# Mixture-of-experts stage of an attention + MoE + FFN kernel: experts taken in an order sorted on the chip, each with a column width of its own, and weights laid out by partition

## The chip, the cores and the metric

One core of one Trainium2 chip runs the whole program. The metric is the device time of that core in microseconds (us). Unchanged, the kernel takes 641.47 us in the median of three runs (641.1 to 641.62).

## What is computed

Three layers follow each other on 1152 tokens of 512 numbers, in float32. First an attention in which each row keeps its 32 largest scores; its output `x` then goes through a mixture of eight experts, and that through a feed-forward layer. Cut to what matters here:

```python
logits = x @ w_gate                        # x is [1152, 512], w_gate [512, 8]
expert_idx = np.argmax(logits, axis=1)     # one expert for each token
gate_w = probs[np.arange(N), expert_idx]
...                                        # disp[e] = the tokens of expert e, in order; at most 288 each
h = np.maximum(np.einsum('ecd,edf->ecf', disp, w1), 0.0)   # w1 is [8, 512, 1024]
y = np.einsum('ecf,efd->ecd', h, w2)                       # w2 is [8, 1024, 512]
out[i] = gate_w[i] * y[expert_idx[i], pos[i]]
...
h = x @ w_in                               # the last layer, w_in [512, 2048]
g = h * np.clip(h + 3.0, 0.0, 6.0) / 6.0
return g @ w_out                           # w_out [2048, 512]
```

How many tokens an expert gets depends on the data. With the reference's inputs at its default seed the eight experts get 72, 137, 101, 181, 115, 186, 186 and 174 tokens.

## The kernel before, in words

The program has three stages one after the other. Within each, the order of the instructions on every engine is that of the source (`manual_schedule`): loops written out with hand-set positions, of which the ones used here are named below.

**Attention and routing.** 72 units (9 tiles of 128 tokens by 8 heads) pass through a software pipeline (`in_steps`). As tiles are done, `route` finds each token's expert (`oh`, one-hot) and its place among that expert's tokens (`pos`), and `send_rows` (L138) scatters the tokens' rows, scaled by their gate, into a DRAM buffer `xs` that holds 1152 rows for every expert. At step 16 the first expert's two weight matrices are loaded into two of three slots (`wslot`, 2 MB each, L600). At the end, for the last two tiles, the first expert's rows don't wait for the scatter: what has landed is read back (`load_first`, L187) and transposed into PSUM (`x_rows`, L161), the rest is added by a product with a 0/1 matrix (`pick0`, `x_pick`, L169), and VectorE copies the sum into `xe0` (`x_copy`, L158), on which the first expert starts. `most` (L512) keeps the count of tokens per expert (`sums`) and its maximum (`top_sum`).

**Experts.** The loop at L863 runs over 8 experts with 16 steps `m` each. `W = 192` columns (token places) are used for every expert. Steps 0 to 7 of an expert (phase a) make `hT = relu(w1' x)`, one 128-row block each, with four products (`hps`, L819), then ScalarE copies out (L827). Steps 8 to 15 (phase b) make the output (`yps`, L819), which ScalarE and VectorE write as a high and a low part into `x2h` and `x2l` at a column that is read from memory at run time (`nums`, L868, L836, L837). Each product of float32 numbers is two passes on TensorE, so an expert has 64 x 2 = 128 passes. In phase b the next expert's rows (`x_load`, L743) are transposed between the products (`turn`, `x_turn`, L153).

All loads are issued by SyncE (SP) in program order. Weight matrix n+3 is loaded into the slot of matrix n as soon as that one's phase is over (L872), so that two whole phases lie between a load's issue and its first use. Each load moves 128 lines: w1 in four pieces of 4 KB, w2 in eight of 2 KB. `x_load` of expert e+3 follows at the end of expert e. Beside these, from step 32 on, `conv_ticks` (L719) turns the last layer's weights, which come as 64-bit numbers, into pairs of float32 parts; one tick goes with every second step, and every third tick sends for the next 512 KB block (`load_raw`, L686): `w_in` blocks in pieces of 1 KB, `w_out` blocks in pieces of 4 KB. `finals` (L178) makes the columns at which the experts' outputs start, `compact` (L768) each token's column, and `check` (L783) sets `again` if an expert has more than 192 tokens or the selection of scores was not exact. If `again` is above 0, L970 runs everything once more in a slow form that has room for any input.

**Last layer.** `up` (L912) and `down` (L927) run over the 1152 columns, while the remaining weight blocks are converted. TensorE's products here have 384 or 512 columns.

Of the kernel before, what the change touches and what calls it, by code (L numbers as in the profile page):

```python
# [44 lines left out]
KW = 11  # L45
FILL = 4
# [11 lines left out]
def topk_attention_moe_ffn_kernel(ctx, tc, qT, kT, vx, vT, wg, w1, w2, w_in, w_out, out, cap):  # L58
# [17 lines left out]
    again = const.tile([1, 1], I32, name="again")  # L76

    def forward(fast):


        W = 192 if fast else cap
# [10 lines left out]
        top_sum = wp.tile([P, 1], F32, name="top_sum")  # L92
# [11 lines left out]
        if fast:  # L104
            x0, x0b, slot1 = (slots[2][:p, at:at + n] for p, at, n in
                              ((P, 0, DM), (W - P, DM, DM), (P, 3 * DM + W, W)))
            plain = slots[2][:, 4 * DM:5 * DM]
            xg_last = {t: wp.tile([P, DM], F32, name=f"xg{t}") for t in (NT - 2, NT - 1)}
            pick0 = {t: slots[2][:, at:at + W] for t, at in ((NT - 1, 3 * DM), (NT - 2, 6 * DM))}
        nload = [0]  # L110

        def load_w(name, part=0, parts=1):
            kind, e = name
# [32 lines left out]
        def x_turn(rows, x, psum):  # L146

            for g in range(2):
# [7 lines left out]
                x_copy(xp, g, x)  # L156

        def x_copy(xp, g, x):  # L158
            nc.vector.tensor_copy(x[:, 2 * g:2 * g + 2, :W], xp[:, :, :W])

        def x_rows(xp):  # L161
            for g in range(2):
                for i in range(2):
                    ks = slice((2 * g + i) * P, (2 * g + i + 1) * P)
                    for r, r0, n in ((x0, 0, P), (x0b, P, W - P)):
                        nc.tensor.matmul(xp[g][:, i, r0:r0 + n], r[:, ks], ident[:n, :n], is_transpose=True,
                                         start=False, stop=False)

        def x_pick(xp, xg, t, start=False, x=None):  # L169
            for g in range(2):  # L170
# [4 lines left out]
                if x is not None:  # L175
                    x_copy(xp[g], g, x)
# [10 lines left out]
        def load_first():  # L187
            nc.sync.dma_start(x0, xs[:P])
            nc.sync.dma_start(x0b, xs[P:W])

        with ExitStack() as actx:
# [74 lines left out]
            if fast:  # L266
                nc.gpsimd.iota(slot1, pattern=[[1, W]], base=1, channel_multiplier=0,
# [244 lines left out]
            def most(tot_p):  # L512
                v = nc.vector
                return [lambda: v.tensor_copy(sums[:, 0], tot_p),
                        lambda: v.tensor_reduce(top_sum, sums[:, 0], axis=AX.X, op=OP.max)]
# [45 lines left out]
            def in_steps():  # L561
# [80 lines left out]
                for f, *args in ((ptr, u - 2), (expo, u - 2), (attv, u - 3), (send, 4), (send, 5), (attv, u - 2),  # L642
# [6 lines left out]
                banks = [pool.tile([P, 2, 512], F32, name=name)[:, 0, :2 * W].rearrange("p (a w) -> p a w", a=2)  # L649
# [10 lines left out]
                    *most(tot)])  # L660
                x_rows(banks)
# [11 lines left out]
        with ExitStack() as mctx:  # L673
# [12 lines left out]
            def load_raw(n):  # L686
                f, j = divmod(n, 2)
                if f < NF:
                    r = raw[n % NRAW]
                    if j:  # L690
                        nc.sync.dma_start(r, w_out[f * P:(f + 1) * P])
                    else:
                        nc.sync.dma_start(r.rearrange("p (a f) -> p a f", a=HP),
                                          w_in[:, f * 2 * P:(f + 1) * 2 * P].rearrange("(a p) f -> p a f", p=P))
# [39 lines left out]
            with ExitStack() as ectx:  # L734
# [3 lines left out]
                PARTS = [(a, min(P, W - a)) for a in range(0, W, P)]  # L738
# [4 lines left out]
                def x_load(e):  # L743
                    xin[e] = []
                    for a, n in PARTS:
                        r = eb.tile([P, DM], F32, name=f"x{a}", bufs=2 + (a == 0))
                        if fast and n < P and e < 3:
                            nc.gpsimd.memset(r[n:], 0.0)
                        nc.sync.dma_start(r[:n], xs[e * NTOK + a:e * NTOK + a + n])
                        xin[e].append((r, a, n))  # L750

                def turn(e):
                    rows = xin.pop(e)
                    xe[e] = eb.tile([P, HP, W], F32, name="xe", bufs=1) if e % 2 else xe0
                    if fast:
                        return x_turn([(r, a, P) for r, a, n in rows], xe[e], two_banks)
                    return turn_one(rows, xe[e])

                def turn_one(rows, x):
                    for k in range(HP):  # L760
# [5 lines left out]
                        nc.vector.tensor_copy(x[:, k], xp)  # L766

# [15 lines left out]
                def check():  # L783
# [14 lines left out]
                    v.scalar_tensor_tensor(again_f, top_sum[:1], float(W), again_f, op0=OP.is_gt, op1=OP.add)  # L798
# [13 lines left out]
                class Expert:  # L812
                    def __init__(self, x, col):
                        self.x, self.col, self.y = x, col, {}
                        self.h = eb.tile([P, NFF, W], F32, name="hT", bufs=2 if fast else 1)

                    def products(self, out, wb, m, first, last):
                        for k in range(HP):
                            nc.tensor.matmul(out, wb[:, k], m[:, k], start=first and k == 0, stop=last and k == HP - 1)  # L819
                            yield  # L820

                    def use(self, wb, what):
                        if what[0] == "a":
                            f = what[1]
                            o = ps.tile([P, W], F32, tag="ps", name="hps")
                            yield from self.products(o, wb, self.x, True, True)
                            nc.scalar.activation(self.h[:, f], o, AF.Relu)  # L827
                            return
                        d, half = what[1:]
                        if half == 0:  # L830
                            self.y[d] = ps.tile([P, W], F32, tag="ps", name="yps")
                        o = self.y[d]
                        yield from self.products(o, wb, self.h[:, half * HP:(half + 1) * HP], half == 0, half == 1)
                        if half == 1:
                            cols = bass.ds(self.col(), W)
# [27 lines left out]
                for m in range(E * NP):  # L863
                    e, r = divmod(m, NP)
                    if r == 0:
                        ex = Expert(xe[e], lambda e=e: offv[e])
# [12 lines left out]
                    if fast and m == FIN:  # L879
                        finals()  # L880
                    if m == CPT:
                        compact()
# [139 lines left out]
```

## Time and profile before

| | us |
|---|---|
| median of 3 runs | 641.47 |
| the profiled execution | 639.62 |
| its span, first to last instruction | 637.8 |
| attention and routing, up to the first expert's product | 0 to 254.4 |
| experts | 254.4 to 427.4 |
| last layer | 427.4 to 637.8 |

The span is the profile's: 1.8 us of the execution lie around it. TensorE is busy for 609.8 us of it, VectorE for 375.5, ScalarE for 360.3, GpSimd for 311.3. In the profile PE is TensorE's matmul row, PEld its weight loads, DVE is VectorE, ACT ScalarE, POOL GpSimd, SP SyncE, and a small q marks an engine's own sequencer. A matmul's row ends when its result has drained, so rows of one stream overlap: the time between two starts, not the length of one row, is what a pass takes from the engine.

### The profile page before, as it was taken

What the parts mean: (1) busy time and instruction counts of PE and PEld (TensorE: products, weight loads), DVE (VectorE), ACT (ScalarE), POOL (GpSimd) and SP (SyncE); (2) the same over time, 40 slices, a digit from 0 to 9 for tenths busy, and PEclk for the clock granted to TensorE, in tenths of its full rate; (3) what the DMA queues carried; (4) which work ended last, traced back from release to release, by engine and by line L of the source; (5) the groups of instructions that cost most, each with busy time, mean ns of one, the idle gap of its engine ahead of it and who ended that gap; (6) DMA issues with size and microseconds to landing.
All of it is one profiled execution on the core that took longest, in us unless ns stands there. A gap on an engine that the chain in (4) does not pass through costs nothing.

```text
span 637.8 us, 12077 instructions
## 1 busy us (share of the span) xinstructions
PE 609.8 (96%) x4096; PEld 549.2 (86%) x4096; DVE 375.5 (59%) x1765; ACT 360.3 (56%) x687; POOL 311.3 (49%) x380
## 2 busy tenths in 40 slices
PE   8999999999888879999999999999999999999994
PEld 4888889888777767999999999999999999999993
DVE  5999999999999994002333323427665664222220
ACT  5999999989999963121334334336555553242221
POOL 7999999979999953001244222124234322030001
PEclk9999999999999979999999999999999999999998
DMA  8549600100000002885889887422222310020001
GB/s 268 168 134 386 212 17 2 35 2 18 18 18 19 2 1 95 293 290 148 306 264 280 276 308 239 165 64 85 81 85 84 97 34 1 1 99 1 1 1 54
DMA packets 36598, 74.13 MB, mean 116 GB/s; under 512 B 4016, under 2 KB 12464, under 8 KB 36528
## 3 DMA queue, kind: packets, MB, share of 16 engines
q1 hardware_dynamic: 34800, 68.55, 32.7%
q0 software_dynamic: 1728, 4.72, 2.0%
q8 instruction: 34, 0.56, 0.3%
q14 instruction: 36, 0.29, 0.2%
HBM read 63.83 MB, written 9.44 MB: 115 GB/s over the span
## 4 chain that ended last, share of the span: by engine, by line
PE 52%; DVE 24%; issue 15%; POOL 6%; ACT 1%; DMA 1%; DVEq 0%; SPq 0%; POOLq 0%; ACTq 0%
PE hps L819 13%; PE yps L819 13%; PE h L916 8%; PE acc L930 7%; DVE lists L342 7%; DVE lists L360 5%; DVE l L369 4%; DVE tops L371 3%; PE av L426 2%; POOL s L356 2%; PE ps L321 2%; PE pt L408 2%; POOL out_dram L939 1%; PE pt L566 1%; PE mix L443 1%
## 5 line engine op out<-in xcount | busy, mean ns | idle before, releaser
L342 DVE MAX8 lists<-s 128x8 f32<-128x72 f32 x576 | 118.6, 220 | 4.1 <-ACT s L326 4.1
L426 PE MATMUL av<-vt,pts 128*128 128x96 f32 (+1 forms) x800 | 100.5, 275 | 0.0
L916 PE MATMUL h<-x2h,fw 128*128 128x384 f32 x384 | 98.3, 336 | 0.9 <-DVE x2l L837 0.9
L426 PEld LDWEIGHTS av<-vt,pts 128*128 128x128 f32 (+1 forms) x800 | 92.1, 184 | 2.1 <-issue 0.9
L356 POOL TENSOR_TENSOR s<-s,cut 128x576 f32<-128x576 f32 x72 | 92.0, 1277 | 3.6 <-ACT cut L353 3.5
L819 PE MATMUL yps<-hT,wslot 128*128 128x192 f32 x512 | 90.9, 326 | 0.0
L930 PE MATMUL acc<-fw,gh 128*128 128x512 f32 x288 | 89.6, 392 | 0.0
L348 POOL TENSOR_TENSOR s<-s,lists 128x576 f32<-128x576 f32 x72 | 83.6, 1162 | 6.1 <-DVE lists L342 3.8
L408 PE MATMUL pt<-ident,ub 128*128 128x128 f32 x360 | 72.6, 287 | 13.5 <-POOL ub L385 7.9
L819 PE MATMUL hps<-xe,wslot 128*128 128x192 f32 x512 | 84.6, 326 | 0.2 <-DVE sc L184 0.2
L819 PEld LDWEIGHTS hps<-xe,wslot 128*128 128x128 f32 x512 | 83.4, 190 | 0.7 <-issue 0.7
L819 PEld LDWEIGHTS yps<-hT,wslot 128*128 128x128 f32 x512 | 82.1, 190 | 1.2
L408 PEld LDWEIGHTS pt<-ident,ub 128*128 128x128 f32 x360 | 50.8, 141 | 33.6 <-POOL ub L385 16.4
L916 PEld LDWEIGHTS h<-x2h,fw 128*128 128x128 f32 x384 | 70.5, 188 | 5.1 <-DVE x2l L837 1.2
L409 PE MATMUL pt<-drop,lb 128*128 128x128 bf16 x360 | 65.7, 220 | 0.0
L916 PE MATMUL h<-x2l,fw 128*128 128x384 f32 x192 | 64.7, 337 | 0.0
L930 PEld LDWEIGHTS acc<-fw,gh 128*128 128x128 f32 x288 | 53.4, 188 | 9.0
L919 ACT ACTIVATE g<-h,three 128x384 f32<-128x384 f32 x48 | 27.9, 581 | 55.7 <-PE h L916 55.7
L920 DVE SCALAR_TENSOR_TENSOR g<-g,h 128x384 f32<-128x384 f32 x48 | 26.5, 551 | 54.3 <-ACT g L919 53.9
L394 ACT ACTIVATE lb<-s,tops 128x576 bf16<-128x576 f32 x71 | 55.0, 775 | 4.9 <-DVE tops L371 2.8
L924 DVE TENSOR_TENSOR gl<-g,gh 128x384 fp32r<-128x384 f32 x48 | 27.4, 571 | 51.0 <-ACT gh L923 51.0
L923 ACT CAST gh<-g 128x384 fp32r<-128x384 f32 x48 | 24.7, 515 | 57.5 <-PE acc L930 52.9
(393 smaller groups left out, 1057.2 us busy)
## 6 DMA issues: line engine op xcount, KB each, us to landing
wslot<-in_w_dram SPq DMA_DIRECT2D x15, 2048.0 KB, 9.3
raw<-in_w_in_dram SPq DMA_DIRECT2D x16, 512.0 KB, 5.0
raw<-in_w_out_dram SPq DMA_DIRECT2D x16, 512.0 KB, 3.6
xs<-x_tok SPq DMA_DIRECT2D x8, 576.0 KB, 13.1
vt<-in_vx_dram SPq DMA_DIRECT2D x8, 365.0 KB, 3.6
kt<-in_kT_dram SPq DMA_DIRECT2D x8, 288.0 KB, 4.5
vts<-in_vT_dram SPq DMA_DIRECT2D x8, 288.0 KB, 3.8
qt<-in_qT_dram SPq DMA_DIRECT2D x9, 256.0 KB, 4.2
```

The lines of the kernel that those rows point to most:

```text
L342: yield lambda c=c: nc.vector.max(lists[t % 2][:, h, c], st[u][:, c * CW:(c + 1) * CW])
L348: nc.gpsimd.tensor_tensor(s2, s, lists[t % 2][:, h, :NCK, KEEP:].to_broadcast([P, NCK, CW]), op=OP.subtract)
L356: nc.gpsimd.tensor_tensor(st2[u], st[u], cuts.pop(u), op=OP.subtract)
L360: nc.vector.max(lists[t % 2][:, h, NCK], st2.pop(u))
L394: nc.scalar.activation(lbufs[u % 2][:, :S], st.pop(u), AF.Relu, bias=tops[t][:, h, TOPK - 1:], scale=-1.0)
L408: nc.tensor.matmul(pt[:, c], ubufs[u % 2][:, cs], ident, is_transpose=True, start=True, stop=False)
L409: nc.tensor.matmul(pt[:, c], lbufs[u % 2][:, cs], drop, start=False, stop=True)
L426: nc.tensor.matmul(av[t, g][rows, h % 4], pts[:, c, cols], vt[b, h // 2][:, at:at + VC], start=c == 0, stop=c == 4)
L819: nc.tensor.matmul(out, wb[:, k], m[:, k], start=first and k == 0, stop=last and k == HP - 1)
L916: nc.tensor.matmul(h2, fw[f][:, 0, a, k * P:(k + 1) * P], (x2h, x2l)[b][:, k, c * CH:(c + 1) * CH], start=n == 0, stop=n == len(ops) - 1)
L919: nc.scalar.activation(g, h2, AF.Relu, bias=three)
L930: nc.tensor.matmul(acc[j], g[a][:, j * P:(j + 1) * P], fw[f][:, 1, b], start=f == 0 and n == 0, stop=f == NF - 1 and n == 2)
```

## The change

The experts' order and widths change, and the layout of the weights in DRAM.

- `order()` sorts the eight experts by token count on VectorE, right after the counts are known. Expert 0 stays first (its weights are loaded long before); the other places take, by `PLACES`, the largest, the smallest, the second largest, the second smallest and so on. It writes the experts' numbers by place into `eids`.
- Place j has `WIDTHS[j]` columns: 176, 192, 132, 192, 140, 188, 152, 176, together 1348, where before there were 8 x 192 = 1536. Products, copies and row loads of a place use its width. With the inputs named above the places hold 72, 186, 101, 186, 115, 181, 137 and 174 tokens. `check` compares each place with its own width.
- Since the expert of a place is known at run time only, SP reads its number from `eids` (`who(j)`, one register load for each of the places 1 to 7) and the loads of weights and rows take their address from that register.
- The host lays `w1` and `w2` out so that what one partition gets is one line of 16 KB, and `w_in` so that its blocks come in lines of 4 KB.
- Small tables are filled on GpSimd at the start (10 instructions more), `finals_fast` and `compact_fast` take the sorted order into account, and the rows that fill up a row tile are cleared whole (128 rows, not the last 64).

```diff
+WIDTHS = (176, 192, 132, 192, 140, 188, 152, 176)
+PLACES = (0, 1, 7, 2, 6, 3, 5, 4)
...
-        W = 192 if fast else cap
+        Ws = WIDTHS if fast else [cap] * E
+        W, W0 = max(Ws), Ws[0]
...
         def load_w(name, part=0, parts=1):
-            src = (w1 if kind == "a" else w2)[e]
-            n = src.shape[1] // parts
+            n = 4096 // parts
             cols = slice(part * n, part * n + n)
-            nc.sync.dma_start(t.rearrange("p (a b) -> p a b", b=src.shape[1])[:, :, cols],
-                              src.rearrange("(a p) f -> p a f", p=P)[:, :, cols])
+            nc.sync.dma_start(t[:, cols], (w1 if kind == "a" else w2)[one(j), :, cols])
+        def one(j):
+            return bass.ds(eid[j], 1) if j in eid else j
...
+        def order():
+            v = nc.vector
+            v.scalar_tensor_tensor(keys, sums[:, 0], float(E), rank, op0=OP.mult, op1=OP.add)
+            v.max(places, keys)
+            v.tensor_copy(keys_in := sizes, places)
+            for j, at in enumerate(PLACES):
+                if j != at:
+                    v.tensor_copy(places[:, j:j + 1], keys_in[:, at:at + 1])
+            v.tensor_copy(whole, places)
+            v.tensor_scalar(eids, whole[:1], E - 1, E - 1, op0=OP.bitwise_and, op1=OP.bitwise_xor)
...
             def most(tot_p):
-                return [lambda: v.tensor_copy(sums[:, 0], tot_p),
-                        lambda: v.tensor_reduce(top_sum, sums[:, 0], axis=AX.X, op=OP.max)]
+                return [lambda: nc.vector.tensor_copy(sums[:, 0], tot_p)]
...
                     *most(tot)])
+                order()
                 x_rows(banks)
...
-                        nc.sync.dma_start(r[:n], xs[e * NTOK + a:e * NTOK + a + n])
+                        nc.sync.dma_start(r[:n], by_expert[one(j), a:a + n])
...
-                            nc.tensor.matmul(out, wb[:, k], m[:, k], start=first and k == 0, stop=last and k == HP - 1)
+                            nc.tensor.matmul(out, wb[:, k], m[:, k, :self.w], start=first and k == 0, stop=last and k == HP - 1)
...
+                def who(j):
+                    if fast and j < E:
+                        eid[j] = nc.values_load(eids[0:1, j:j + 1], engines=(mybir.EngineType.SP,), min_val=0,
+                                                max_val=E - 1)
                 if fast:
+                    who(1)
                     load_w(stream[2], 0, 2)
                     x_load(1)
                     load_w(stream[2], 1, 2)
+                    who(2)
...
                         if e + 3 < E:
+                            who(e + 3)
                             x_load(e + 3)
...
+    rows_first = lambda w: w.reshape(E, -1, P, w.shape[2]).transpose(0, 2, 1, 3).reshape(E, P, -1)
```

How the change moves VectorE's instructions at the end of the routing: the stretch from the count of tokens to the copy of the first expert's rows. `xe` is the first expert's input, `ps` and `pt` the two PSUM banks it is summed in. Before:

```order
L514 COPY sums<-tot_p 128x8
L515 TENSOR_REDUCE top_sum<-sums 128x1
L491 TENSOR_SCALAR rd<-cm 128x1
L492 TENSOR_TENSOR ra<-pos_p,oh 128x8
L493 TENSOR_REDUCE pr<-ra 128x1
L494 TENSOR_TENSOR dest<-rd,pr 128x1
L159 COPY xe_86<-ps 128x384
L159 COPY xe_86<-pt 128x384
```

After the change the eleven instructions of `order()` stand before the two copies, and one reduction is gone:

```order
L551 COPY sums<-tot_p 128x8
L529 TENSOR_SCALAR rd<-cm 128x1
L530 TENSOR_TENSOR ra<-pos_p,oh 128x8
L531 TENSOR_REDUCE pr<-ra 128x1
L532 TENSOR_TENSOR dest<-rd,pr 128x1
L193 SCALAR_TENSOR_TENSOR keys<-sums,rank 128x8
L194 MAX places<-keys 128x8
L195 COPY sizes<-places 128x8
L198 COPY places<-sizes 128x1 x6
L199 CAST whole<-places 128x8
L200 TENSOR_SCALAR eids<-whole 1x8
L171 COPY xe_93<-ps 128x2x176
```

The copies of the first expert's rows moved behind the sort on VectorE, and each of them has 352 columns where it had 384.

How it moves SP's queue at the start of the experts (`in_w` stands for the experts' weights, `x` for an expert's rows). Before:

```order
L189 DMA wslot_89<-xs 64x512
L121 DMA wslot_89<-in_w_dram 128x4x512
L749 DMA x_4196<-xs 128x512
L749 DMA x_4198<-xs 64x512
L121 DMA wslot_89<-in_w_dram 128x4x512
L693 DMA raw_4183<-in_w_in_dram 128x4x256
```

With the change:

```order
L222 DMA wslot_96<-xs 48x512
L897 TENSOR_LOAD eids
L897 ISA x2
L128 ISA
L128 DMA wslot_96<-in_w_dram 128x2048
L784 ISA
L784 DMA x_4233<-xs 128x512
L784 ISA
L784 DMA x_4235<-xs 64x512
L128 ISA
L128 DMA wslot_96<-in_w_dram 128x2048
L897 TENSOR_LOAD eids
```

A register load that waits for the sort now stands ahead of the second expert's weights, and a short address instruction (ISA) ahead of every load whose expert is found at run time; the order of the loads themselves is the same.

## Rows read from the trace of the kernel before

**Rows 1.** Experts: stretch, length, PE/PEld/DVE/ACT/POOL busy (instructions), clock, DMA share, GB/s.
```profile
254.40:427.40 173.00, 172.99 (x1081) 171.49 (x1081) 50.34 (x117) 55.36 (x141) 39.07 (x43) 1.00 0.74 243
```
**Rows 2.** Line L819, the experts' products: weight loads and matmuls, ns min/median/max.
```profile
L819 PEld LDWEIGHTS hps<-xe,wslot x512: 186/190/191, 254.4 to 416.5; 128*128 128x128 f32 x171
L819 PE MATMUL hps<-xe,wslot x512: 326/326/401, 254.4 to 416.7; 128*128 128x192 f32 x171
```
**Rows 3.** Chain of waits around the third expert: start us, us, what, how many.
```profile
298.03 10.40 PE hps L819 x64
308.43 0.33 PE yps L819 x2
308.76 0.11 PE xp L153
...
312.03 7.80 PE yps L819 x48
```
**Rows 4.** Attention's products of 96 columns, ten passes in order of time.
```profile
228.06 1.31 PE L426 MATMUL av<-vt,pts 128*128 128x96 f32 x10
```
**Rows 5.** The same products and their weight loads, among the page's costliest groups.
```profile
L426 PE MATMUL av<-vt,pts 128*128 128x96 f32 (+1 forms) x800 | 100.5, 275 | 0.0
...
L426 PEld LDWEIGHTS av<-vt,pts 128*128 128x128 f32 (+1 forms) x800 | 92.1, 184 | 2.1 <-issue 0.9
```
**Rows 6.** VectorE in order of time, end of the routing.
```profile
250.30 0.16 DVE L515 TENSOR_REDUCE top_sum<-sums 128x1 f32<-128x8 f32 x1
250.37 0.14 DVE L491 TENSOR_SCALAR rd<-cm 128x1 f32<-128x1 f32 x1
...
250.62 0.16 DVE L493 TENSOR_REDUCE pr<-ra 128x1 f32<-128x8 f32 x1
250.82 0.16 DVE L494 TENSOR_TENSOR dest<-rd,pr 128x1 int32<-128x1 f32 x1
252.95 0.56 DVE L159 COPY xe<-ps 128x384 f32<-128x384 f32 x1 [1.97 <-PE ps L173]
```
**Rows 7.** TensorE behind the experts' last product, in order of time.
```profile
424.81 2.60 PE L819 MATMUL yps<-hT,wslot 128*128 128x192 f32 x15
428.28 0.62 PE L916 MATMUL h<-x2h,fw 128*128 128x384 f32 x2 [0.87 <-DVE x2l L837]
```
**Rows 8.** SP's DMA issues at the start of the experts, in order of time.
```profile
253.64 0.38 SPq L121 DMA_DIRECT2D wslot<-in_w_dram  x1
259.51 0.85 SPq L749 DMA_DIRECT2D x<-xs  x2
```
**Rows 9.** The row loads issued at 259.5 (second expert), issue to landing.
```profile
DMA to landing us min/median/max: 2.8/2.8/2.8
```
**Rows 10.** Register loads of line L868, ns min/median/max.
```profile
L868 ACTq TENSOR_LOAD <-nums x8: 275/279/477, 265.1 to 417.1; - x8
```
**Rows 11.** The weight load (w1) issued at 298.1, issue to landing.
```profile
DMA to landing us min/median/max: 12.0/12.0/12.0
```
**Rows 12.** The weight load (w2) issued at 286.8, issue to landing.
```profile
DMA to landing us min/median/max: 8.3/8.3/8.3
```
**Rows 13.** Busy time of the experts at places 2, 3, 4 and 6 (columns as in rows 1).
```profile
297.70:319.50 21.80, 21.80 (x139) 21.62 (x138) 7.29 (x21) 6.49 (x17) 4.84 (x7) 1.00 0.78 236
319.50:341.20 21.70, 21.70 (x138) 21.53 (x137) 7.71 (x17) 8.75 (x21) 9.28 (x12) 1.00 0.91 278
341.20:362.90 21.70, 21.70 (x139) 21.52 (x138) 7.39 (x16) 7.82 (x20) 6.03 (x6) 1.00 0.93 292
...
384.60:406.30 21.70, 21.70 (x138) 21.53 (x138) 7.67 (x17) 8.75 (x21) 5.08 (x4) 1.00 0.79 267
```
**Rows 14.** End of the attention: where the clock fell, and after (columns as in rows 1).
```profile
226.00:232.70 6.70, 3.82 (x57) 3.66 (x58) 6.18 (x22) 4.52 (x10) 4.87 (x6) 1.00 0.01 2
232.70:239.60 6.90, 6.34 (x33) 5.82 (x33) 6.66 (x46) 4.09 (x7) 1.32 (x3) 0.51 0.00 0
...
247.00:254.40 7.40, 5.99 (x45) 4.29 (x45) 4.85 (x27) 1.71 (x4) 1.09 (x2) 1.00 0.25 89
```

More of the change, by code (lines that the diff above doesn't have):

```diff
@@ L45 @@
 KW = 11
+FRONT = 1 << 14
+WIDTHS = (176, 192, 132, 192, 140, 188, 152, 176)
+PLACES = (0, 1, 7, 2, 6, 3, 5, 4)
 FILL = 4
@@ L91, in forward @@
         sums = wp.tile([P, 3, E], F32, name="sums")
-        top_sum = wp.tile([P, 1], F32, name="top_sum")
+        rank, places, most_of = (wp.tile([P, E], F32, name=name) for name in ("rank", "places", "most_of"))
+        keys, sizes, starts = (wp.tile([P, E], F32, name=name) for name in ("keys", "sizes", "starts"))
+        whole = wp.tile([P, E], I32, name="whole")
         gates = wp.tile([P, NT, 1], F32, name="gates")
@@ L144, in send_rows, with x_turn @@
             return sd
-        def x_turn(rows, x, psum):
+        def x_turn(rows, x, psum, w=W):
             for g in range(2):
@@ L175, in x_pick, with finals_fast @@
                 if x is not None:
-                    x_copy(xp[g], g, x)
+                    x_copy(xp[g], g, x, W0)
+        def order():
[8 more added lines that the diff above has]
+            v.tensor_scalar(eids, whole[:1], E - 1, E - 1, op0=OP.bitwise_and, op1=OP.bitwise_xor)
+        def finals_fast():
+            v = nc.vector
+            v.tensor_scalar(whole, whole, 3, 2047, op0=OP.logical_shift_right, op1=OP.bitwise_and)
+            v.tensor_copy(sizes, whole)
+            v.memset(sums[:, 2], 0.0)
+            v.memset(sc[:, 0, 0:1], 0.0)
+            v.tensor_tensor_scan(sc[:, 0, 1:], sizes, sums[:, 2], 0.0, op0=OP.add, op1=OP.add)
+            v.tensor_copy(nums, sc[:1, 0, :E])
         def finals():
@@ L755, in turn @@
                     if fast:
-                        return x_turn([(r, a, P) for r, a, n in rows], xe[e], two_banks)
+                        return x_turn([(r, a, P) for r, a, n in rows], xe[e], two_banks, Ws[e])
                     return turn_one(rows, xe[e])
@@ L766, in turn_one, with compact_fast @@
                         nc.vector.tensor_copy(x[:, k], xp)
+                def compact_fast():
+                    v = nc.vector
+                    same = eb.tile([P, E, E], F32, name="same", bufs=1)
+                    cp = eb.tile([P, NT, E], F32, name="cp", bufs=1)
+                    cs = eb.tile([P, NT], F32, name="cs", bufs=1)
+                    v.tensor_tensor(same, places[:, None, :].to_broadcast([P, E, E]),
+                                    keys[:, :, None].to_broadcast([P, E, E]), op=OP.is_equal)
+                    v.tensor_tensor(same, same, sc[:, 0, None, :E].to_broadcast([P, E, E]), op=OP.mult)
+                    v.tensor_reduce(starts, same, axis=AX.X, op=OP.add)
+                    v.tensor_tensor(cp, pos, starts[:, None, :].to_broadcast([P, NT, E]), op=OP.add)
+                    v.tensor_tensor(cp, cp, oh, op=OP.mult)
+                    v.tensor_reduce(cs, cp, axis=AX.X, op=OP.add)
+                    v.tensor_copy(cposi, cs)
                 def compact():
@@ L1001 @@
     vx = vx.reshape(P, B, 5, HP, 2 * VS).transpose(0, 1, 3, 2, 4)
+    rows_first = lambda w: w.reshape(E, -1, P, w.shape[2]).transpose(0, 2, 1, 3).reshape(E, P, -1)
+    w_in = inputs["moe2_w_in"].reshape(HP, P, F2 // P, P).transpose(2, 1, 0, 3).reshape(F2, DM)
     arrays_in = [
```

76 lines of the change are left out of this document (41 added, 35 removed).

## The prediction

> **What bounds the kernel now.** I read first the busy times by stage: in the 173.0 us of the experts TensorE is busy for 172.99, VectorE for 50, ScalarE for 55, GpSimd for 39, and the DMA engines for a share of 0.74 [rows 1]. So TensorE sets the end of this stage, and the reader should see that nothing else there is near its limit except, in places, the DMA. The chain of waits, read next, says the same: it runs through the products alone, 64 passes of phase a in 10.40 us, and in phase b pairs of passes with a transpose of 0.11 us between, then 48 passes in 7.80 us [rows 3]. 10.40 / 64 and 7.80 / 48 both give 0.1625 us for a pass of 192 columns.
>
> The question on which all else rests is whether a pass with fewer columns is shorter. Each pass also loads 128 columns of weights, and that row lasts 0.19 us, longer than the pass takes [rows 2]; the weight-load row is busy for 171.49 of 173.0 us [rows 1]. Two rows with the same weights and fewer moving columns answer it. The transposes move 128 columns and take 0.11 us each in the chain [rows 3]. Attention's products move 96 columns: ten take 1.31 us, of which the last one's row is 0.275 [rows 4, 5], so one starts (1.31 - 0.275) / 9 = 0.115 us after the other, although their weight load is still a row of 0.184 us [rows 5]. So the weight load hides behind the pass down to about 0.11 us, and above that the pass goes by its columns. From 128 to 192 columns the step is (0.1625 - 0.11) / 64 = 0.82 ns a column; in plain proportion it would be 0.1625 / 192 = 0.85 ns. By the first slope the narrowest place, 132 columns, takes 0.113 us a pass, just at the end of the ground that these rows cover (0.11 to 0.115).
>
> The Trainium skill says otherwise in "Perfetto Trace Analysis", section "Identifying the Most-Contended Engine": headroom on TensorE is judged by the busy share of the weight loads, not of the matmuls. That share is 99% here [rows 1], so by that rule the stage would stand at its limit whatever the columns, and the sum below would be about nothing. The ten passes at 0.115 us [rows 4] speak against it; it is the first rival.
>
> **The change, part by part.**
>
> *Narrower products.* 128 passes for each place, and 1536 - 1348 = 188 columns less over the eight: 24,064 pass-columns at 0.82 to 0.85 ns, 19.7 to 20.4 us. All of it lies on the path, since TensorE doesn't wait in this stage. I take 20.0. The transposes keep their 128 columns and number. Copies out of PSUM by ScalarE and VectorE get shorter; they are off the path.
>
> *The sort.* `order()` puts eleven instructions ahead of the copy of the first expert's rows, which is on the path: TensorE starts the experts when the two copies are done. Before, VectorE was through at 250.98 and sat idle for 1.97 us until TensorE had the sum [rows 6]. The removed reduction gives back 0.07 us (the next one started that much later). Instructions that need each other start 0.20 us apart (250.62, 250.82), those that don't 0.07 (250.30, 250.37) [rows 6]. Eleven of them take 0.8 to 2.2 us, so the sort ends between 251.7 and 253.1, where the copy started at 252.95: a delay of 0 to 0.2 us. I take 0.1, since five of the six small copies don't need each other. The products that make these rows go from 192 to 176 columns: eight passes on the path, 16 x 0.82 ns each, 0.1 us back. Together nothing.
>
> *The number of the expert, read by SP.* Seven register loads, 0.28 to 0.48 us each by the nearest row [rows 10], and a short address step ahead of each load. They stand in SP's queue. The first waits for the sort, 253.1 at the latest, so the second expert's first weights leave at about 253.9 at the latest, not 253.64 [rows 8]. What is queued behind: the second expert's rows, which wait for the scatter anyway until 259.51 [rows 8]. These rows are the narrowest place of the plan. They land 2.8 us after issue [rows 9], the second part at about 262.8, and TensorE wants them from phase b of the first expert on, which comes at 254.4 + 64 x 0.149 = 264.0, not 264.8. So 1.2 us of cover is left; without it TensorE would wait out the difference. Cost nothing; bounds 0 to 0.5.
>
> *Layout.* The bytes are the same, in longer lines. A w1 load (lines of 4 KB, its four pieces 512 KB apart) took 12.0 us to land [rows 11], a w2 load 8.3 [rows 12]; with one layout for both I expect 8 to 9, and 12 at worst. TensorE waited for neither, so this is worth nothing by itself; how far the cover shrinks is the second rival.
>
> *End of the stage.* TensorE waited 0.87 us for the last `x2l` [rows 7], behind conversions on ScalarE and VectorE whose length doesn't change. The last 15 passes, 2.60 us now [rows 7], get 15 x 16 x 0.82 ns = 0.2 us shorter, so up to that much of the gain comes back as a longer wait. I take 0.1.
>
> *Everything else* (tables on GpSimd at the start, the cleared rows, the three instructions more in the check, the sums by place) lies on engines that are idle for over two thirds of the stage [rows 1] or at the start. Nothing.
>
> **Sum:** -20.0 + 0.0 + 0.1 = -19.9 us. Against the profiled execution, 639.62 us with a span of 637.8, that is 619.7; the median of the runs lies 1.85 us above that execution, at 641.47, so I forecast **621.6 us**.
>
> **The rivals.**
>
> 1. *Weight loads bind, no gain.* The case of the rule above: the pass stays at 0.1625 us and the time at about 641.5. For it: 0.19 us rows, 99% busy. Against: the same loads at 0.115 and 0.11 us a pass [rows 3, 4]. Chance 0.02.
>
> 2. *The DMA becomes the bound in the narrow places.* Place 4 moves 292 GB/s x 21.7 us = 6.34 MB at a DMA share of 0.93 [rows 13], so about 310 GB/s is what the engines gave at full share. With 140 columns it lasts 128 x 0.120 + 0.9 (its eight transposes) = 16.2 us, which asks for 391 GB/s. At 310 it takes 20.4: 4.2 us lost. Places 2 (236 GB/s x 21.8 us = 5.14 MB in 15.4 us) and 6 (267 x 21.7 = 5.79 MB in 17.5) would lose 1.2 each: 6.6 in all, 628.2 us. Against it: a load is issued two phases ahead, and the wide places between have room (place 3: 6.03 MB, 19.5 us of DMA in 21.7). The tightest load is the first one of place 3, issued when place 1 ends and needed when place 2 is through, 15.4 us later; its like took 12.0 [rows 11]. If the pieces 512 KB apart are what makes the w1 load slow, the new layout takes the slow part away, and I would give this rival 0.08. The Trainium skill's "DMA: Bandwidth & Descriptors", section "Latency and other measured facts", has a row pitch of 512 KB at 207 GB/s where the full rate was 214, and only pitches of megabytes far below; by that rule the pitch is not what makes the w1 load slower than the w2 load [rows 11, 12], and it may stay so. No row here tells what does, so I don't count on the better case. Chance 0.14, most of it with a loss of 2 to 4 us.
>
> 3. *Slower: the long lines are read badly.* One mechanism, in the weight loads: a line of 16 KB goes to one DMA engine whole, eight lines an engine, at addresses found at run time; if what holds up the w1 load [rows 11] holds up these lines too, its slow rate becomes the rule. 2.1 MB in 12.0 us [rows 11] is 175 GB/s; the stage's 243 GB/s x 173 us = 42 MB [rows 1] would take 240 us, 67 more than now: 708 us. It makes the kernel slower as soon as the rate falls below those 243 GB/s. For it: no row shows lines of 16 KB. Against: lines of 2 KB that lie next to each other land in 8.3 us [rows 12], and these lie next to each other too. Chance 0.03.
>
> 4. *A stretch at half clock.* At 232.7 the granted clock fell to 0.51 for 6.9 us (the level of 1.2 GHz, not 2.4), after 6.7 us in which TensorE was busy for 57% [rows 14]. Just ahead of the experts it is busy for 5.99 of 7.40 us, 81%, at full clock; the change takes away some 0.2 us there, 78%. If the clock falls anyway, the stretch costs 6.9 x 0.49 = 3.4 us: 625.0. Chance 0.03.
>
> 5. *The change doesn't do what it says.* A place with more tokens than its width sets `again` and the whole slow form runs: more than twice the time. With the reference's inputs the sorted sizes 72, 186, 101, 186, 115, 181, 137, 174 are under the widths 176, 192, 132, 192, 140, 188, 152, 176 everywhere. Chance 0.01.
>
> **How the numbers follow.** My forecast has 0.77, the rivals 0.02, 0.14, 0.03, 0.03 and 0.01. The forecast's own range is 620.4 to 622.6: gain 19.7 to 20.4 with the bounds of the sort, of the first rows and of the end, and some tenths for the run. The range reaches on through the case of half clock to 625.4, which takes in about half of the DMA case; what is left out above is some 0.13. Faster by over 0.2% (about what a measurement of this kernel tells from no change): forecast, DMA and clock, 0.94. Same: rival 1, 0.02. Slower: rivals 3 and 5, 0.04.
>
> **What would show it.** In the changed profile: 64 passes of `hps` in 10.40 us at 192 columns, 7.3 at 132, 7.7 at 140 and 9.6 at 176 in the chain; the experts' stage 153 us long, TensorE busy throughout; the first copy of `xe` not later than 253.15; weight loads that land in 8 to 9 us (12 would leave 3.4 us of cover at place 3) at a DMA share near 0.8; the last layer unchanged in length. I am wrong if passes at 132 columns don't go below 0.13 us (rival 1), or if TensorE's wait for `wslot` or, through ScalarE, for `raw` takes more than 1 us in places 2, 4 or 6 (rival 2).

## The result, and the profile after it

The changed kernel took **621.06 us** in the median of four runs (620.54 to 623.47), beside 641.29 for the kernel before: a ratio of 0.9696 [0.9683, 0.971], 20.2 us faster. Two later sets of five runs of the same kernel gave 625.53 and 626.49 (below). What an execution can lose is most of what follows; why the first set lost least is not shown. The profiled execution is one of the first four, 621.33 us with a span of 619.5.

| profiled execution, us | before | after |
|---|---|---|
| span | 637.8 | 619.5 |
| first product of the experts | 254.41 | 253.91 |
| first product of the last layer | 428.28 | 410.92 |
| between the two ("the stage" from here on) | 173.87 | 157.01 |
| from there to the end | 209.48 | 208.60 |

So 16.9 of the 18.3 us come from the stage; 0.5 lie ahead of it and 0.9 behind it. The busy times by stage, with columns as in [rows 1] (the whole stage, then places 3 and 4):

```profile
253.90:410.00 156.10, 153.43 (x1081) 152.14 (x1081) 48.85 (x121) 53.55 (x141) 39.09 (x43) 1.00 0.81 267
...
310.70:333.90 23.20, 22.22 (x141) 21.74 (x139) 9.00 (x20) 9.03 (x22) 9.98 (x13) 1.00 1.01 271
333.90:351.70 17.80, 16.14 (x134) 15.99 (x135) 5.64 (x13) 6.45 (x17) 6.02 (x6) 1.00 1.01 344
```

TensorE is idle for 2.7 us, which it was not before, and at places 3 and 4 the DMA engines are at their full share. The chain of waits shows the shorter passes, and what the idle time is (start us, us, what):

```profile
295.83 7.20 PE hps L871 x64
...
305.83 5.40 PE yps L871 x48
311.23 10.41 PE hps L871 x64
...
321.66 21.63 DMA wslot<-in_w_dram
```

At 132 columns 64 passes take 7.20 us and 48 take 5.40, both 0.1125 a pass, against 0.1625 in [rows 3]. Behind place 3 the chain no longer runs through products but through a weight load that was issued at 321.66 and landed 21.63 us later. TensorE in order of time shows that both matrices of place 4 (140 columns) came late:

```profile
334.24 7.87 PE L871 MATMUL hps<-xe,wslot 128*128 128x140 f32 x64 [1.31 <-DMA wslot<-in_w_dram]
343.43 0.48 PE L871 MATMUL yps<-hT,wslot 128*128 128x140 f32 x2 [1.32 <-DMA wslot<-in_w_dram]
```

A phase is counted below from its first product to the next one's, so these waits stand at the ends of place 3's second and place 4's first phase: 12.77 and 9.19 us, where 11.29 and 7.63 were needed (seen in `e12_late_again`, a run without waits), 3.0 us in all. The weight loads landed later than forecast and spread wider (first all of them, then the one issued at 295.86):

```profile
L128 SPq DMA_DIRECT2D wslot<-in_w_dram x15: 332/342/367, 253.5 to 381.8; - x15
...
DMA to landing us min/median/max: 5.8/10.8/17.6
...
DMA to landing us min/median/max: 14.6/14.6/14.6
```

The other places that the prediction spoke of answer to [rows 6], [rows 8] and [rows 7]. VectorE in order of time, from the sort's first instruction to the first copy:

```profile
250.63 0.16 DVE L193 SCALAR_TENSOR_TENSOR keys<-sums,rank 128x8 f32<-128x8 f32 x1
...
251.93 0.16 DVE L200 TENSOR_SCALAR eids<-whole 1x8 int32<-1x8 int32 x1
252.53 0.52 DVE L171 COPY xe<-ps 128x352 f32<-128x352 f32 x1 [0.44 <-PE ps L185]
```

SP's issues in order of time:

```profile
253.53 0.37 SPq L128 DMA_DIRECT2D wslot<-in_w_dram  x1
259.72 1.61 SPq L784 DMA_DIRECT2D x<-xs  x2
```

TensorE behind the experts' last product:

```profile
410.92 0.62 PE L976 MATMUL h<-x2h,fw 128*128 128x384 f32 x2 [0.95 <-DVE x2l L889]
```

The sort ended at 252.09, and VectorE still waited 0.44 us for TensorE's sum: it cost nothing. SP's first load left at 253.53. The wait at the end of the stage is 0.95 us, where it was 0.87.

### The profile page after: what moved, and what is told of

It is laid out like the page before. It is cut to its first block, busy times and chain, and to the rows that moved or that the text cites. A ratio compares the mean times of both kernels' runs of the same rounds, so it can differ in the third digit from the quotient of the medians.

```text
span 619.5 us, 12180 instructions
## 1 busy us (share of the span) xinstructions
PE 587.6 (95%) x4096; PEld 527.0 (85%) x4096; DVE 375.3 (61%) x1776; ACT 358.9 (58%) x687; POOL 311.9 (50%) x390
## 4 chain that ended last, share of the span: by engine, by line
PE 42%; DVE 27%; issue 16%; POOL 7%; DMA 4%; ACT 2%; DVEq 0%; POOLq 0%; ACTq 0%
PE hps L871 11%; PE yps L871 10%; DVE lists L380 9%; PE h L976 9%; PE acc L990 8%; DVE lists L398 6%; DVE l L407 5%; DMA wslot<-in_w_dram 3%; DVE tops L409 3%; POOL s L394 2%; POOL s L386 1%; POOL out_dram L999 1%; DVE tops L405 1%; PE av L464 1%; DVE x_tok L472 1%
## 5 line engine op out<-in xcount | busy, mean ns | idle before, releaser
L464 PE MATMUL av<-vt,pts 128*128 128x96 f32 (+1 forms) x800 | 98.3, 272 | 0.0
L464 PEld LDWEIGHTS av<-vt,pts 128*128 128x128 f32 (+1 forms) x800 | 89.9, 181 | 2.0 <-issue 0.9
L446 PE MATMUL pt<-ident,ub 128*128 128x128 f32 x360 | 71.8, 285 | 14.6 <-POOL ub L423 8.0
L871 PE MATMUL yps<-hT,wslot 128*128 128x176 f32 (+5 forms) x512 | 80.9, 307 | 1.3 <-DMA wslot<-in_w_dram 1.3
L871 PEld LDWEIGHTS yps<-hT,wslot 128*128 128x128 f32 x512 | 74.5, 190 | 2.1 <-ACT hT L879 1.5
L871 PE MATMUL hps<-xe,wslot 128*128 128x176 f32 (+5 forms) x512 | 74.6, 307 | 1.5 <-DMA wslot<-in_w_dram 1.3
L871 PEld LDWEIGHTS hps<-xe,wslot 128*128 128x128 f32 x512 | 73.5, 190 | 2.2 <-DVE x2l L889 1.6
## 6 DMA issues: line engine op xcount, KB each, us to landing
wslot<-in_w_dram SPq DMA_DIRECT2D x15, 2048.0 KB, 11.5
```

The lines of the kernel that those rows point to most:

```text
L446: nc.tensor.matmul(pt[:, c], ubufs[u % 2][:, cs], ident, is_transpose=True, start=True, stop=False)
L464: nc.tensor.matmul(av[t, g][rows, h % 4], pts[:, c, cols], vt[b, h // 2][:, at:at + VC], start=c == 0, stop=c == 4)
L871: nc.tensor.matmul(out, wb[:, k], m[:, k, :self.w], start=first and k == 0, stop=last and k == HP - 1)
```

## What slows the loads: scatters of 4-byte numbers

While TensorE works on the experts, GpSimd sends nine scatters of row numbers (`name_rows`, 128 numbers of 4 bytes each) at steps 34 to 66. Two of them, and then the DMA queues from 296 to 304 us, just behind them:

```profile
293.30 0.97 POOL L857 DMA_INDIRECT ids<-tok,cposi  x1 [36.96 <-DVE cposi L815]
...
294.58 0.97 POOL L857 DMA_INDIRECT ids<-tok,cposi  x1 [0.22 <-issue]
```
```profile
DMA packets 55, 0.38 MB, mean 47 GB/s; under 512 B 32, under 2 KB 32, under 8 KB 32
...
q1 hardware_dynamic: 23, 0.38, 83.7%
q0 software_dynamic: 32, 0.00, 0.3%
```

In these 8 us, 23 lines of 16 KB kept the 16 engines busy for 83.7% and moved 0.38 MB: 8 us x 16 x 0.837 / 23 = 4.7 us a line. The same stretch in a run with the scatters elsewhere (`e12_late_again`), where 218 packets took less of the engines' time:

```profile
DMA packets 219, 2.23 MB, mean 279 GB/s; under 512 B 15, under 2 KB 15, under 8 KB 92
...
q1 hardware_dynamic: 218, 2.22, 76.0%
```

The scatters themselves are short packets; what stretches is every other transfer near them. The Trainium skill's "DMA: Bandwidth & Descriptors", section "SWDGE vs HWDGE vs iDMA", says that the two kinds of queue are different ones inside an engine, taken in turn; by that a line would wait for a short packet at most, and the rows here, 4.7 us a line, show that more is lost.

## The experiments

All ratios are to the kernel before, run beside them. "Late numbers" means the scatters moved to steps 105 to 121. "Loss" is the stage less 153.9 us, the shortest seen at these widths, in the one profiled execution of each set. It is waits for weights, but for 0.5 us in e1 and 0.2 each in e4 and e7, where the first place starts at half clock, and 1.6 in e11 (below).

| run | median us (lowest to highest) | ratio [interval] | stage | loss |
|---|---|---|---|---|
| the change, first set | 621.06 (620.54 to 623.47) | 0.9696 [0.9683, 0.971] | 157.01 | 3.1 |
| e7, the change again | 625.53 (623.51 to 627.51) | 0.9749 [0.9729, 0.9769] | 158.29 | 4.4 |
| e11, the change a third time | 626.49 (624.84 to 630.68) | 0.978 [0.9753, 0.9807] | 160.35 | 6.4 |
| e9, code shifted | 623.31 (622.39 to 627.0) | 0.9724 [0.9698, 0.9751] | 159.51 | 5.6 |
| e4, old lines | 626.82 (622.37 to 628.03) | 0.9751 [0.9718, 0.9783] | 158.43 | 4.5 |
| e1, late numbers | 619.62 (619.38 to 620.19) | 0.9662 [0.9649, 0.9675] | 154.44 | 0.5 |
| e12, late numbers again | 619.77 (618.69 to 620.05) | 0.9658 [0.9645, 0.9671] | 153.91 | 0 |
| e10, late numbers, code shifted | 619.44 (618.9 to 620.79) | 0.9659 [0.9646, 0.9672] | 153.98 | 0.1 |
| e6, late numbers, more dummies | 620.32 (619.0 to 620.97) | 0.9668 [0.9654, 0.9681] | 154.03 | 0.1 |
| e8, late numbers, old lines | 620.46 (619.85 to 621.12) | 0.9677 [0.9663, 0.9692] | 153.91 | 0 |
| e2, all places 192 | 640.95 (639.15 to 643.98) | 1.0005 [0.9986, 1.0023] | 174.11 | |
| e3, before with late numbers | 641.41 (640.32 to 642.35) | 1.0001 [0.9991, 1.0011] | 173.87 | |

**Scatters later (e1, e12, and e3 on the kernel before).**

```diff
-NS, NG, IE = 34, 4, 6
+NS, NG, IE = 105, 2, 127
...
-                    if e == IE and r == 0:
+                    if m == IE:
```

> The changed kernel with its nine scatters of row numbers (ids, name_rows) moved from steps 34 to 66 to steps 105 to 121, and the load that reads them back to step 127. Theory A, the scatters of 4-byte numbers hold up the weight loads behind them: the slow spells of the DMA at 295 to 304, 315 to 320 and 325 to 340 us go, weight loads of places 2 to 5 land in 6 to 10 us instead of up to 17.6, TensorE's wait for wslot (2.6 us) goes, and the time falls by 2.5 to 4 us to about 618, with less spread between runs. Theory B, the narrow places simply ask for more than the DMA gives: the spells and the wait stay where they are and the time stays at 621 within 1 us.

> Late numbers alone again, the control: 619.4 to 621.0 us. By theory D it too can start late in some execution, since its code ahead of 250 us is the changed kernel's (15 runs of three kernels with late numbers had none above 621.2): a run at 622 to 626 us would show that late numbers give no protection; none would leave that open.

> The kernel before with the scatters of row numbers moved as in e1. Theory A: the w1 load that took 12.0 us to land now takes 8 to 9, like w2's, although its lines and their pitch are the old ones; the time stays at 641.3 within 1 us, since TensorE waited for no load. If the old layout made w1 slow: it still takes about 12.

In both sets of late numbers TensorE's waits for `wslot` are gone, so theory A stands. e1 gains 1.4 us on the first set of the change, less than expected, and e12 6.7 on e11, more; what it takes away differs from one execution of the change to the next. All of e1's loss is a first place at half clock. The whole stage of e12, its DMA from 336.2 to 344.2 us, and its weight loads:

```profile
254.90:408.80 153.90, 152.95 (x1081) 152.12 (x1081) 49.90 (x123) 54.08 (x142) 39.62 (x43) 1.00 0.78 268
...
336.20:344.20 8.00, 8.00 (x70) 8.00 (x70) 2.68 (x6) 4.51 (x11) 2.98 (x3) 1.00 0.99 392
```
```profile
DMA to landing us min/median/max: 5.5/9.4/12.1
```

The slow spell went with the scatters. In e1 it comes from 388 to 396 us, at 75 GB/s and a share of 0.88, where the last weights are all but in:

```profile
388.00:396.00 8.00, 8.00 (x57) 8.00 (x56) 3.40 (x7) 4.05 (x11) 5.59 (x9) 1.00 0.88 75
```

In the kernel before the edit changes no time, since TensorE waited for no load there; but its w1 load issued at 299.0 now lands in 7.7 us, where the like of it took 12.0 [rows 11]:

```profile
DMA to landing us min/median/max: 7.7/7.7/7.7
```

This answers what the prediction had to leave open, as far as one profile of each kernel can: the scatters ahead of it made that load slow, not its pieces 512 KB apart. The row on the pitch in the Trainium skill's "DMA: Bandwidth & Descriptors", section "Latency and other measured facts", which spoke against the pitch, agrees with that; it was measured for the distance from one partition's row to the next, and here it is pieces of one partition that lie 512 KB apart.

**Only the columns undone (e2).** `WIDTHS = (192,) * 8`; sort, register loads, layout and order stay.

> The changed kernel with all eight widths at 192: sort, register loads, layout and order of the experts stay. If the gain is the columns alone: the time of the kernel before, 641.3 within 1 us, experts' stage 173 us, no wait for wslot. If the layout or the order of the experts gives part of the gain: under 640. If sort and register loads cost something that the columns hide: 642 or more.

The time is that of before. So the other parts together give and cost nothing beyond the 1.5 us that the interval leaves; the gain is the columns.

**Only the layout of `w1` and `w2` undone, with early and with late numbers (e4, e8).** `w_in` keeps its new layout.

```diff
-            n = 4096 // parts
+            src = w1 if kind == "a" else w2
+            n = src.shape[2] // parts
...
-            nc.sync.dma_start(t[:, cols], (w1 if kind == "a" else w2)[one(j), :, cols])
+            nc.sync.dma_start(t.rearrange("p (a b) -> p a b", b=src.shape[2])[:, :, cols],
+                              src[one(j) if j in eid else slice(j, j + 1)].rearrange("e (a p) f -> p (e a) f", p=P)[:, :, cols])
```

> The changed kernel with w1 and w2 laid out as before (w1 in lines of 4 KB, w2 of 2 KB), read with the expert's number from a register; w_in keeps its new layout. If the long lines matter little (theory A, the scatters set the stall): 621 within 1.5 us, wait for wslot 1 to 5 us. If the layout is what keeps the DMA ahead of the narrow places: the wait grows to over 6 us and the time to 625 or more.

> The changed kernel with the weights in the old layout (4 KB and 2 KB lines) and late numbers. Theory A, the layout is worth nothing by itself and only the scatters cost cover: no wait for weights, the experts' stage takes 154.0 to 155.0 us as with late numbers alone, and the time is within 1 us of it. Theory B, the old lines' lower rate binds where the products are narrow: waits for wslot of 1 to 3 us in places 2 to 4 remain though the scatters are gone from there, and the stage takes 155.5 to 157.5 us.

With late numbers the old lines wait for nothing: 153.91 us, the same stage as the long lines. With early ones they lose 4.5 us, within what the long lines lose (3.1 to 6.4). At the time e4 alone looked like a cost of the old lines; e7 and e11 took that reading away. The layout is worth nothing that these runs can show.

**How far a pass follows its columns (e5).** Late numbers and 104 columns at place 2, which holds 101 tokens (so no row is left out after all; only the test for a size is). One run, 617.95 us.

```diff
-WIDTHS = (176, 192, 132, 192, 140, 188, 152, 176)
+WIDTHS = (176, 192, 104, 192, 140, 188, 152, 176)
...
-                    v.tensor_tensor(again_f, again_f, big[:, E:], op=OP.add)
```

> Late numbers and the changed kernel's layout, with 104 columns in place 2 instead of 132; the rows of that expert beyond its 104th are left out, and so is the test for a size above its place's width. Theory A, a pass is as long as its columns: the 64 passes of the first product of place 2 took 7.20 us at 132 columns and those of place 6 and of 176 columns 8.27 (152) and 9.55 us (176), 0.053 us per column, so they take 7.20 - 28 x 0.053 = 5.7 us. Theory B, the load of the weights sets a floor (it was counted busy nearly all through the stage): 7.0 to 7.2 us again. In the second product of the place the four transposes of a second piece of rows go too, so it is read only as a check: 6.1 to 6.3 us by A, above 7.2 by B. If the weights' transfer binds at that pace instead, the passes stay at 5.7 us and a wait for wslot shows in place 3.

The chain of waits at place 2:

```profile
295.39 7.12 PE hps L870 x64
...
305.18 5.34 PE yps L870 x48
```

0.111 us a pass, where 132 columns take 0.1125: the time of theory B. From 192 down to 132 columns the pass follows its columns (64 passes take 10.40 us at 192, 10.19 at 188, 9.55 at 176, 8.27 at 152, 7.63 at 140 and 7.20 at 132: 0.83 ns a column and pass), and below that it stops. That the weight load is what sets this floor no run shows by itself; its row was busy for 99% at 192 columns as well [rows 1]. So the rule of the Trainium skill's "Perfetto Trace Analysis", section "Identifying the Most-Contended Engine", that the weight loads' busy share tells the headroom, can hold here from about 132 columns down at most: above that the share was 99% and the stage still got 11.5% shorter.

**The changed kernel again (e7), and a late start.**

> The changed kernel itself, unedited, beside the run of late numbers and others on one chip: 620.5 to 623.5 us. If the 3.0 us of waiting for weights are a matter of the scatters of row numbers, its phases show it again in the second product of place 3 and the first of place 4, 2 to 4 us in sum; if they were a chance of one execution, they are elsewhere or gone.

Its median is 625.53. The stage loses 4.4 us, 4.2 of them to waits for weights at places 3 and 4, the same places as before; they were no chance of one execution. The rest is a start at 258.93, not 253.91. TensorE ahead of the experts:

```profile
249.07 0.37 PE L539 MATMUL tot_p<-oh,ones 128*128 128x8 bf16 x9
252.22 1.33 PE L178 MATMUL ps<-ident,wslot 128*128 128x128 f32 x4 [2.79 <-DMA wslot<-xs]
```

It waits 2.79 us for rows (0.24 in the first profile), and after that works at half clock (granted 0.57 from 255 to 260): from the rows' arrival to the experts' first product it takes 6.71 us, not 4.12, so about half of the 5.0 us is the clock. The rows were late because SP could issue their load only when the last scatter of rows had landed: 249.39, not 247.11. The scatters' landings, first in the first profile, then in e7:

```profile
DMA to landing us min/median/max: 2.7/2.8/2.8
```
```profile
DMA to landing us min/median/max: 2.7/3.8/4.8
```

What the DMA moved from 245.9 to 249.0, in 40 slices, again first in the first profile:

```profile
GB/s 476 317 264 476 370 423 264 106 0 0 0 211 0 0 0 0 0 0 0 0 0 0 0 0 0 0 0 0 185 211 344 344 291 185 132 159 370 317 344 264
```
```profile
GB/s 0 0 370 581 423 317 423 264 476 264 264 0 0 0 0 0 0 0 0 0 0 0 0 0 0 0 53 0 0 0 0 53 0 0 53 0 53 0 0 0
```

In the first the scatter is through in one go, and the lone slice of 211 is a packet of the instruction queue (16 KB) behind it; the rows' load follows. In e7 that packet is in flight among the scatter's last ones, and four of those (the slices of 53) trickle in up to 248.8. e4 started late too (258.40), in the same way; the other nine profiles at the new widths did not, and in none of them does this packet lie among the scatter's last. That the packet is the cause is read from this coincidence.

**Shifting the code (e9, e10), with the change as control (e11).** Dummy products near 12 to 20 us in quarters: 96 instructions more on TensorE, as many columns.

```diff
-                                keep_warm(FILL, wm)
+                                keep_warm(4 * FILL, wm, P)
```

> The changed kernel with the 16 dummy products of 512 columns near 12 to 20 us written as 64 of 128 columns: as many columns, but 96 instructions more on TensorE ahead of the routing, by which every 16 KB instruction packet (TensorE's code, one every 15.8 us there) comes at an earlier place of the program, some 6 us here. Theory D: the changed kernel starts its experts at 253.9 or at 258.9 us according to whether the instruction packet of about 246 us falls behind or among the last packets of the scatter of rows that the first expert's rows wait for; moved to about 241 us it meets none, the experts start at 253.5 to 255.5 us in the profiled execution, and no run is above 622.5 us: median 620.5 to 622.0. Rival: the late start has nothing to do with that packet, and runs of 623.5 to 627.5 us turn up as often as in the unedited kernel beside it. In either case the 3.0 us of waiting in places 3 and 4 stay.

> Late numbers and the shifted code together. By theory D there is nothing left to wait for but a stretch at half clock: 618.5 to 620.0 us, none above 621. By its rival the shift does nothing here: the same median as late numbers alone, within 0.5 us.

> The changed kernel unedited, the control for the two shifted ones: 620.5 to 627.5 us, in two groups, one at 620.5 to 621.5 (start of the experts at 253.9) and one at 623.5 to 627.5 (start near 258.9); theory D says that its profiled execution, if it starts late, has the instruction packet of about 246 us ahead of the last packets of the scatter, and if it starts early, behind them.

In e9 the packet came at 242.1 and the experts started at 254.90, as theory D has it; but its sum failed, 623.31 and not 620.5 to 622.0, for 5.6 us of waits for weights (3 were expected). In e11 the packet lay behind the scatter and the start was early (254.27), again as D has it, but the time was 624.84: the stage lost 6.4 us. Of these 4.8 are waits at places 3 and 4. The other 1.6 come behind the longest of them, 3.00 us, where TensorE works at half clock (granted 0.50 from 346 to 348), and the same pairs of passes take 0.47 us and then 0.24:

```profile
322.02 23.42 DMA wslot<-in_w_dram
345.44 0.14 issue
...
347.27 0.47 PE yps L871 x2
...
349.10 0.24 PE yps L871 x2
```

Behind e4's wait of 2.88 us at the same place the clock stayed at 1.00. So the late start explains e7's profile and e4's, but two sets were slow without it in their profile, by waits for weights; how the executions that were not profiled divide is not known. With late numbers the shift did nothing for the time (619.44 beside 619.77); the packet, at 243.5 there, lay among the packets of an earlier scatter, which took 4.7 us to land but was through at 245.5, before it was needed. Five sets with late numbers, 24 timed runs, had none above 621.2; four sets with early numbers besides the first, 19 runs, had none below 622.3. Three of the first set's four runs lie at 620.54 to 621.33: why so low, no run shows. Whether late numbers also keep the start early isn't settled, as no reason for it is known.

**Half clock (e6).** `warm(3)` ahead of the last `route_now`, with late numbers.

> Late numbers plus three dummy products of 512 columns ahead of the last tile's count, where TensorE stood idle for 0.85 us: what is left between this kernel and the forecast is the stretch at half clock. Theory C: the clock falls at about 252 us because TensorE did too little just ahead of it; with its idle time filled the granted clock of 245 to 260 us is 1.00, the experts start at 253.9 us or before, and the median is 617.5 to 619.0 with less spread. Rival: the clock falls once in some place of the routing whatever three products do; then it still shows a stretch at 0.5 of 3.4 or 6.8 us somewhere between 230 and 260 us, and the median is 619.4 to 620.5, or above where the products themselves hold up the count.

The rival: TensorE was busier just ahead (4.28 of 5 us, 3.71 in e1), and the clock still fell (columns as in [rows 1]):

```profile
245.00:250.00 5.00, 4.28 (x42) 3.52 (x41) 3.15 (x18) 1.71 (x4) 0.68 (x5) 1.00 0.36 128
250.00:255.00 5.00, 4.91 (x18) 3.06 (x18) 3.27 (x21) 0.00 (x0) 1.99 (x3) 0.69 0.28 74
```

Among the profiles without a late start, the stretch lies at 232 to 240 us (e8, e10, e11, e12), at 250 to 256 (e1, e6, e9), or is missing (the first profile and e5). Those that have it start the experts at 254.27 to 255.01, those without it at 253.91 and 253.92: they start 0.4 to 1.0 us later where it lies at 232 to 240, and 1.0 to 1.1 where it lies at 250 to 256; in e1 it reaches into the first place and costs 0.5 more there. Why it falls where it does stays open.

## Why the prediction was right, and where it was not

The time was forecast at 621.6 and came out at 621.06, in the range; the later sets, 625.53 and 626.49, lie just above its top of 625.4. Step by step:

- **Narrower products, -20.0 us: right.** Without waits (e8, e12) the stage shrinks from 173.87 to 153.91, by 19.96; the sum had -19.9 with the end. The choice to read the floor of a pass from [rows 3] and [rows 4], not from the weight loads' share, was what decided this, and e5 finds the floor at 0.111 us where they had put it (0.11). Rival 1 is gone.
- **Sort, register loads, end of the stage, nothing: right.** The first copy came at 252.53 (253.15 was the limit) and SP's load left at 253.53. The wait at the end grew by 0.08 us, not 0.1.
- **Layout, worth nothing by itself: right; loads landing in 8 to 9 us, 12 at worst: wrong.** The median was 10.8 and single loads took 17.6 and 21.6. The step "with one layout for both I expect 8 to 9" took the slow w1 load [rows 11] for a matter of lines, or left it open; it was the scatters, which the sum did not name.
- **No wait for weights in the sum: wrong**, by 3.1 us in the first profile and 4.2 to 5.6 in others. By the prediction's own sign ("more than 1 us in places 2, 4 or 6") rival 2 came true beside the forecast: TensorE waited 1.31 and 1.32 us for the two matrices of place 4, and it was not "busy throughout". Rival 2 had the wait: "most of it with a loss of 2 to 4 us", the largest part at place 4. Its place and price were near. Its cause was not: it took 310 GB/s for what the engines can give, but e12 moved 392 GB/s at a share of 0.99 from 336.2 to 344.2 us and loaded the same bytes with no wait. What was missing is a stretch of up to 8 us behind a group of scatters in which hardly anything lands. In the kernel before a load had 21.7 us from issue to use, and that hid it. Across the narrow place 2 it has 15.4: the load issued at 295.86 took 14.6 of them, and the queue that built up behind it was paid at place 4, where the load issued at 321.66 took 21.63. The chance of 0.14 was too low.
- **Half clock (rival 4), 3.4 us: too dear ahead of the experts, and not looked for elsewhere.** There it cost 0.4 to 1.1 us, some 1.5 in e1, and the kernel before had paid for it too [rows 14]. What rival 4 left out is a stretch behind a wait: 2.6 us of e7's late start, 1.6 us of e11's stage.
- That 621.6 and 621.06 agree so well owes something to chance. Against the profiled execution the forecast was 619.7 and the time 621.33: 3.1 us of waits, less 0.5 of an earlier start and 0.9 in the last layer (208.4 to 209.4 us in the other profiles at the new widths; why is not known). And the medians were taken to lie 1.85 us above the profiled execution, which after the change is itself 0.27 above the median.

The best version found is the change with late numbers: on one chip 619.77 us, beside 626.49 for the change itself and 641.46 for the kernel before, so 6.7 and 21.7 us less.

## What to carry to other kernels

A pass gets shorter with its columns until a floor is reached (0.111 us here), and that floor can be read from narrow products of the same kind in the trace; the weight loads' busy share alone does not tell it. A wait can cost more than its length, when the clock falls behind it. When a change makes the consumer faster, ask of each transfer that was hidden what its worst landing is and what stands beside that one in time: an unexplained 12 us among loads of 8 is a term of the sum. Small scattered writes belong where no large load is in flight, or behind the last one.

## What was not expected of the hardware

A scatter of 128 numbers of 4 bytes slows the loads in flight beside it for microseconds: lines of 16 KB took 4.7 us on average where the DMA was busy for 83.7%, and the rate fell to 47 GB/s. In e7 and e4, the two profiles in which one 16 KB packet of the instruction queue lay among the last packets of the scatter of rows, the experts started 5.0 and 4.5 us later than in the first profile; in e7 that scatter landed in 4.8 us, not 2.8. Both effects differ from execution to execution, and profiles of the same kernel lost 3.1 us, 4.4 and the late start, and 6.4; why the sets' medians lie as they do, 621.06 and then 625.53 and 626.49, these profiles do not settle.
